# Packed attention and two MoE layers on one core: smaller normalization, p laid out by transposes, finer slots, new planner constants

## The chip, the cores and the metric

The kernel runs on one core of one Trainium2 chip. The metric is the device time of one execution in microseconds; the median of several runs is compared. The engines are TensorE (PE, with its weight loads as PEld), VectorE (DVE), ScalarE (ACT), GpSimd (POOL) and SyncE (SP), whose queue issues every DMA here.

## The reference

```python
p_packed = sm_attn(p, k, v)                    # 8 batches x 8 heads, 32 packed queries, 576 keys, head size 64
x = sm_attn(q, p_packed, p_packed)             # 576 queries attend to 32 packed rows
x = x.transpose(0, 2, 1, 3).reshape(4608, 512)
h = x @ w_in                                   # 512 -> 1024
solu = h * softmax(h)
ln = (solu - mean(solu)) / sqrt(var(solu) + 1e-06) * g_ln
x = ln @ w_out                                 # 1024 -> 512
r = maximum(x @ w2_in, 0)                      # 512 -> 2048
out = (r * r) @ w2_out                         # 2048 -> 512
```

The weights arrive as 64-bit numbers and are decoded on the chip. `sm_attn` is a softmax with scale 1/8, its maximum subtracted and 1e-9 added to its sum.

## The kernel before

Three stages follow each other, with overlap at their joins.

**Attention and first MoE** (0 to some 545 us). A unit is four heads of one batch, 16 units in all. `pack` loads p, k, q and v of a unit, transposes them on VectorE, forms the scores of p against k (`s1_mm`, four heads at once, which needs p as a block-diagonal matrix `pb`: a transpose `pT` and a product with a mask, L475 and L478), and packs. `unpack` forms the scores of q against the packed rows, their softmax, and `G`, the packed rows times `w_in`. From the sixth unit on (`whole` is false for the other eleven), operands are split into a high and a low part: ScalarE casts the high part (`hi_op`, L373), VectorE or POOL subtracts it for the low part (`lo_op`, L376), and a product is three matmuls (L391 to L393). `h_tile` forms `ph` for 128 tokens, 36 tiles in all, and normalizes it: maximum (L688), its sign (L689), exponential with its sum (L692), product with the mean (L696), a Square on ScalarE with its sum into `ph` (L700), two small operations that turn the sum `se` into `den` (L704, L705), their addition (L707), a power on POOL (L709), two small operations for scale and bias (L711, L713), and the scaling (L715). Its transposed result is `v`. `y_stage` multiplies it by `w_out`, 18 times, four times 24 products each, and stores y. At the start `load_w_in` decodes four chunks of `w_in` (L406 to L425), `load_w_out` then four of `w_out`, each with the gain `g_sb` multiplied in. In their slots and in spare time the weights of the second MoE are decoded and their sums stored (`prepare`).

**First pass of the second MoE** (`z_group`, to some 940 us). Seven products per group (a scheme with sums of blocks in place of an eighth product), six blocks of 768 tokens with eight groups each. `load_y` loads y as `yr` and splits it. ScalarE copies a product from its bank into an SBUF tile `gw` (L914), VectorE adds others (L918), a square with relu ends it (L923, or L926 and L927), and a DMA stores it in `g_dram`. `gw` takes seven slots in turn: two of its own and five in the space of the `w_out` tiles. ScalarE and VectorE also decode the last weights meanwhile (`w2raw`, `wx`, `wh`).

**Second pass** (`o_products`, to the end). It loads `ga` from `g_dram` and weights `oi`, splits (`cb`), and forms seven products of 8 steps per block of 768 tokens; results gather in `osb` and are stored.

What stands where is decided by a planner. Each step is an operation with an engine, a duration, an urgency (`at`) and the buffers that it reads and writes. `Plan.order` plays the engines through with these durations, a latency from an engine to the next (`hop`, plus 100 ns after ScalarE and VectorE, plus 2000 ns for a DMA to land) and the urgencies, and emits instructions in the order that comes out. On the chip each engine then takes its own in that order, each waiting for its inputs by semaphores. SP's DMAs stand in one such order too.

## Time and profile before

| what | value |
| --- | --- |
| median of 3 runs | 1304.53 us (1303.44 to 1305.07) |
| profiled execution | 1314.35 us |
| its span, first to last instruction | 1312.5 us |
| mean granted TensorE clock | 0.971 |
| busy: PE, DVE, ACT, POOL | 1234.8, 965.8, 777.4, 266.9 us |
| DMA traffic | 218.10 MB, mean 166 GB/s |

Durations are those of the profiled execution, which is 9.8 us above the median of the runs. A timeline row gives start, duration, engine, line, operation and tiles, and in brackets the engine's idle time before it with what ended it. Matmul rows show a latency: the next matmul starts before the last has ended. A granted clock of 1.00 is the 2.4 GHz level and 0.50 the 1.2 GHz level.

### The profile page before, as it was taken

Reading aid. Unit: us, or ns where it says so; the run is one execution under the profiler, and the core shown is the slowest. Engines: PE = TensorE matmul, PEld = TensorE weight load, DVE = VectorE, ACT = ScalarE, POOL = GpSimd, SP = SyncE. Lnnn points to the kernel's source line nnn. Section 1 sums busy time; section 2 is a strip of 40 time slices with the busy share of each in tenths; the row PEclk is TensorE's granted clock in tenths of the full one; section 3 lists DMA queues with packets and bytes.
Section 4 is the critical chain, followed back from the end, with each engine's and each line's share of the span. In section 5 each row is a group of like instructions: output and inputs, shape, how many; then the busy total and the mean of one; then the engine's idle time right before and its main releaser. Section 6 shows DMA issues by size and latency. Waiting matters only on the chain.

```text
span 1312.5 us, 23577 instructions
## 1 busy us (share of the span) xinstructions
PE 1234.8 (94%) x8420; PEld 1138.7 (87%) x8420; DVE 965.8 (74%) x1963; ACT 777.4 (59%) x1606; POOL 266.9 (20%) x269
## 2 busy tenths in 40 slices
PE   4778999999999999899898999999799999999997
PEld 2436889788888888899898999999699999999997
DVE  6998787878888864536676777673488787978885
ACT  2566667667767666557676667565455545555452
POOL 1456555555555542000000000000000000000000
PEclk7797999999999999899999999999899999999999
DMA  7642344353454336856665575735996344444511
GB/s 233 197 121 83 120 144 145 116 163 117 124 152 132 98 112 205 303 191 215 211 202 182 188 248 180 241 136 184 311 391 178 104 143 139 133 141 119 152 42 49
DMA packets 176677, 218.10 MB, mean 166 GB/s; under 512 B 22960, under 2 KB 147376, under 8 KB 175792
## 3 DMA queue, kind: packets, MB, share of 16 engines
q1 hardware_dynamic: 176560, 216.60, 52.4%
q8 instruction: 66, 1.08, 0.3%
q14 instruction: 51, 0.42, 0.1%
HBM read 130.55 MB, written 85.98 MB: 165 GB/s over the span
## 4 chain that ended last, share of the span: by engine, by line
PE 62%; DMA 8%; DVE 6%; ACT 5%; issue 2%; POOL 0%; SPq 0%; DVEq 0%; ACTq 0%; POOLq 0%
PE px L391 7%; PE px L393 7%; PE px L392 7%; PE ph L682 6%; DMA g_dram<-gw 5%; PE pa L391 5%; PE pa L392 5%; PE pa L393 5%; PE py L391 4%; PE py L392 4%; PE py L393 4%; PE ptv L727 2%; DVE gw L918 1%; DMA w2raw<-in_moe_w_out_dram 1%; PE pg L611 1%
## 5 line engine op out<-in xcount | busy, mean ns | idle before, releaser
L373 ACT CAST cb<-ga 128x384 fp32r<-128x384 f32 x336 | 167.4, 513 | 177.0 <-PE px L393 78.1
L376 DVE TENSOR_TENSOR cb<-ga,cb 128x384 fp32r<-128x384 f32 x336 | 181.1, 555 | 66.0 <-ACT cb L373 61.6
L391 PE MATMUL py<-v,wo 128*128 128x256 f32 x576 | 167.7, 291 | 0.2 <-ACT v L373 0.2
L392 PE MATMUL py<-v,wo 128*128 128x256 f32 x576 | 163.9, 285 | 0.3 <-DVE v L376 0.3
L393 PE MATMUL py<-v,wo 128*128 128x256 f32 x576 | 163.7, 284 | 0.0
L391 PE MATMUL px<-y,zi 128*128 128x384 f32 x384 | 134.4, 350 | 17.8 <-ACT gw L914 13.4
L391 PE MATMUL px<-oi,cb 128*128 128x256 f32 x504 | 142.2, 282 | 2.2 <-ACT cb L373 2.2
L393 PE MATMUL px<-oi,cb 128*128 128x256 f32 x504 | 142.4, 283 | 1.5 <-DVE cb L376 1.5
L392 PE MATMUL px<-oi,cb 128*128 128x256 f32 x504 | 142.0, 282 | 0.0
L391 PE MATMUL pa<-oi,cb 128*128 128x256 f32 x504 | 141.5, 281 | 0.0
L392 PE MATMUL pa<-oi,cb 128*128 128x256 f32 x504 | 141.5, 281 | 0.0
L393 PE MATMUL pa<-oi,cb 128*128 128x256 f32 x504 | 141.5, 281 | 0.0
L392 PE MATMUL px<-y,zi 128*128 128x384 f32 x384 | 131.7, 343 | 0.5 <-DVE y L376 0.4
L393 PE MATMUL px<-y,zi 128*128 128x384 f32 x384 | 131.3, 342 | 0.0
L391 PEld LDWEIGHTS py<-v,wo 128*128 128x128 f32 x576 | 111.1, 193 | 7.9 <-issue 6.0
L392 PEld LDWEIGHTS py<-v,wo 128*128 128x128 f32 x576 | 111.4, 193 | 1.1 <-DVE v L376 0.5
L393 PEld LDWEIGHTS py<-v,wo 128*128 128x128 f32 x576 | 111.1, 193 | 0.0
L871 DVE TENSOR_TENSOR ga<-ga 128x384 f32<-128x384 f32 x192 | 100.3, 552 | 4.0 <-DMA ga<-g_dram 3.1
L914 ACT COPY gw<-px 128x384 f32<-128x384 f32 x144 | 66.6, 473 | 61.2 <-PE px L393 35.9
L391 PEld LDWEIGHTS px<-oi,cb 128*128 128x128 f32 x504 | 96.0, 190 | 2.5 <-ACT cb L373 2.5
L393 PEld LDWEIGHTS px<-oi,cb 128*128 128x128 f32 x504 | 96.0, 190 | 1.9 <-DVE cb L376 1.9
L391 PEld LDWEIGHTS px<-y,zi 128*128 128x128 f32 x384 | 73.4, 191 | 26.2 <-ACT gw L914 21.1
(193 smaller groups left out, 3241.6 us busy)
## 6 DMA issues: line engine op xcount, KB each, us to landing
g_dram<-gw SPq DMA_DIRECT2D x192, 192.0 KB, 2.6
ga<-g_dram SPq DMA_DIRECT2D x96, 384.0 KB, 3.6
zi<-z_dram SPq DMA_DIRECT2D x28, 512.0 KB, 6.4
oi<-o_dram SPq DMA_DIRECT2D x24, 512.0 KB, 9.7
kr<-in_k_dram SPq DMA_DIRECT2D x16, 576.0 KB, 4.1
qr<-in_q_dram SPq DMA_DIRECT2D x16, 576.0 KB, 4.2
y_dram<-ysb SPq DMA_DIRECT2D x72, 128.0 KB, 1.8
yr<-y_dram SPq DMA_DIRECT2D x12, 768.0 KB, 6.5
```

What stands on the lines that cost most here:

```text
L373: plan.op(ACT, c_act(cols, sbuf=r[0].pool not in (psm, psh, pso)), at, lambda: nc.scalar.copy(out_(), in_()), r=r, w=w)
L376: plan.either(on(cols, *engines), at, lambda e: vec[e].tensor_tensor(out_(), in_(), hi_().bitcast(F32), op=ALU.subtract), r=r, w=w, port=i ...
L391: nc.tensor.matmul(ps, lh, rh, start=first, stop=False, skip_group_check=onto)
L392: nc.tensor.matmul(ps, lh, rl, start=False, stop=False, skip_group_check=onto)
L393: nc.tensor.matmul(ps, ll, rh, start=False, stop=last, skip_group_check=onto)
L611: nc.tensor.matmul(pg()[es, :], ppq()[:, es], wi[2 * g + e]()[:, fs], start=True, stop=True)
L682: nc.tensor.matmul(ph()[:, fs], al[l]()[:, g], g_tiles[b, g]()[:, r, fs], start=ends[0] and g == 0 and t == 0, stop=ends[1] and g == NG - ...
L727: nc.tensor.transpose(pt()[:, c * P:(c + 1) * P], e()[:, (4 * t + c) * P:(4 * t + c + 1) * P], ident)
L871: plan.op(DVE, c_dve(cols), at, lambda: nc.vector.tensor_tensor(out_(), in0(), in1(), op=op), r=r, w=w, port=True)
L914: plan.op(ACT, c_act(HN), at, lambda: nc.scalar.copy(t(), ps()[:, :HN]), r=[ps], w=[t])
L918: plan.op(DVE, c_dve(HN), at, lambda: nc.vector.tensor_tensor(t(), ps()[:, :HN], t(), op=ALU.add), r=[t, ps], w=[t])
```

## The change

- In `h_tile` the maximum is negated by the reduction itself; `den` is made by one Square on ScalarE, with `dbias` as bias, in place of L704 and L705; the constant factor of the scale goes into `g_neg`, which takes the place of `g_sb`, so that the scale is `rst` itself and L711 goes. Four VectorE operations per tile go, one of ScalarE comes.
- The block-diagonal p stands in three buffers `pbz` that are set to zero once. In the first five units four transposes of 32 partitions write its blocks; in the others one transpose stays, and each block is split by a cast on ScalarE and a subtraction on VectorE.
- `SIN` moves the sign of the `w_in` decoding from VectorE (one shift) to ScalarE (two passes of 1024 columns per chunk).
- The `w_out` tiles of the first two columns are halved, which gives `gw` eleven slots in place of seven, and `osb` two tiles in place of one.
- `hop` and the landing time of a DMA get new numbers, and so do the urgencies of every stage; the load of g for the second pass, its weights, the first pass's weights, stores and the decoding of the last weights get urgencies of their own.

Core of the diff:

```diff
-        return 0 if a == b == PE else 400 if a == PE else 230 if b == PE else 140
+        return 0 if a == b == PE else (260, 130, 110, 70, 40)[a] + (20 if b == PE else 0)
...
-                heapq.heappush(events, (self.span + (100 if e in (ACT, DVE) else 0) + o.lag, i, "done"))
+                heapq.heappush(events, (self.span + o.lag, i, "done"))
...
-    QA, GA, HA, TR, UN = 48.13, 170.05, 35.49, -24.27, 16.33
+    QA, GA, HA, TR, UN = 58.08, 149.76, 25.69, -23.7, 14.51
...
-    WD, WDS, WIS = 106.33, 128.75, 19.54
+    WD, WDS, WIS = 99.51, 140.949, 19.42
...
-    SIN, SOUT = DVE, ACT
+    SIN, SOUT = ACT, ACT
...
-    SUB, KLO = (POOL,), (POOL,)
+    SUB, KLO, ALO = (POOL,), (POOL,), (POOL,)
+    YB, ZL, OL, GL0, GL1, GL2, PS, CS = 138.73, 119.42, 25.08, 15.29, 10.0, 16.72, -26.16, 142.32
...
+    dbias = const.tile([P, 1], F32, name="dbias")
+    nc.gpsimd.memset(dbias, 1e-9 * (1e-6 * F1) ** 0.5)
...
+    g_neg = const.tile([P, C1], F32, name="g_neg")
+    nc.scalar.mul(g_neg, g_sb, -float(F1) * float(F1) ** 0.5)
...
-        plan.op(DMA, max(430.0, nbytes / 358.0), at, lambda: nc.sync.dma_start(out=out_(), in_=in_()), r=r, w=w, lag=2000)
+        plan.op(DMA, max(430.0, nbytes / 358.0), at, lambda: nc.sync.dma_start(out=out_(), in_=in_()), r=r, w=w, lag=2200)
...
-    wo = [[wo_v.tile([P, C1, P], F32R, f"wo{d}{s}") for s in range(2)] for d in range(CD)]
...
+    wo = [[[wo_v.tile([P, C1 // 2, P], F32R, f"wo{d}{s}{h}") for h in range(2)] if d < 2 else [wo_v.tile([P, C1, P], F32R, f"wo{d}{s}")]
+           for s in range(2)] for d in range(CD)]
...
-            xv(), xv(), g_sb.unsqueeze(2).to_broadcast([P, C1, P]), op=ALU.mult), r=[x], w=[x], port=True)
-        split(at, C1 * P, x, *wo[d], vs=lambda t: t.rearrange("p (c d) -> p c d", c=C1))
+            xv(), xv(), g_neg.unsqueeze(2).to_broadcast([P, C1, P]), op=ALU.mult), r=[x], w=[x], port=True)
+        for h, (hi, lo) in enumerate(zip(*wo[d])):
+            n = C1 // len(wo[d][0])
+            split(at, n * P, x, hi, lo, vs=lambda t, h=h, n=n: t.rearrange("p (c d) -> p c d", c=C1)[:, h * n:(h + 1) * n])
...
+    pbz = [ab.tile([P, 2, HG, 32], F32 if i == 0 else F32R, f"pbz{i}") for i in range(3)]
...
-        pT = ab.tile([P, 2, 32], F32, "pT", tag="s", bufs=2)
-        plan.op(DVE, c_dve(64), at, lambda: nc.vector.transpose(
-            out=pT(), in_=pr().rearrange("p (e i) -> p e i", e=2)), r=[pr], w=[pT])
-        pb = ab.tile([P, 2, HG, 32], F32, "pb", tag="pbl") if whole else ab.tile([P, 2, HG, 32], F32, "pb", tag="s", bufs=2)
-        plan.either(on(256, DVE), at, lambda e: vec[e].tensor_tensor(
-            pb(), pT().unsqueeze(2).to_broadcast([P, 2, HG, 32]),
-            mask.unsqueeze(1).unsqueeze(3).to_broadcast([P, 2, HG, 32]), op=ALU.mult), r=[pT], w=[pb], port=True)
-        pbs = [pb]
-        if not whole:
-            pbs = [ab.tile([P, 2, P], F32R, n) for n in ("pbh", "pbl")]
-            split(at, 256, pb, *pbs, vs=lambda t: t.rearrange("p e h n -> p e (h n)"))
+        pbs = pbz[:1] if whole else pbz[1:]
+        if n in (0, NX):
+            for t in pbs:
+                plan.op(ACT, c_act(256), at - 30, lambda t=t: nc.scalar.copy(
+                    t().rearrange("p e h n -> p e (h n)"), zero.to_broadcast([P, 2, P])), w=[t])
+        if whole:
+            for h in range(HG):
+                plan.op(DVE, c_dve(64), at, lambda h=h, ps=slice(32 * h, 32 * h + 32): nc.vector.transpose(
+                    out=pbs[0]()[ps, :, h], in_=pr()[ps].rearrange("p (e i) -> p e i", e=2)), r=[pr], w=pbs)
+        else:
+            pT = ab.tile([P, 2, 32], F32, "pT", tag="s", bufs=2)
+            plan.op(DVE, c_dve(64), at, lambda: nc.vector.transpose(
+                out=pT(), in_=pr().rearrange("p (e i) -> p e i", e=2)), r=[pr], w=[pT])
+            for h in range(HG):
+                split(at, 64, pT, *pbs, (DVE,), vs=lambda t, h=h: t[32 * h:32 * h + 32], vo=lambda t, h=h: t[32 * h:32 * h + 32, :, h])
...
-        ppT = ab.tile([P, 2, HG, NP], F32, "ppT", **(dict(tag="pbh") if whole else dict(tag="s", bufs=2)))
+        ppT = ab.tile([P, 2, HG, NP], F32, "ppT", **(dict(tag="pth") if whole else dict(tag="s", bufs=2)))
...
-                    split(at + HA, cs.stop - cs.start, a_tiles[b, g], *al, vs=view, vo=to)
+                    split(at + HA, cs.stop - cs.start, a_tiles[b, g], *al, ALO, vs=view, vo=to)
...
-        plan.op(DVE, c_dve(F1), at + 1, lambda: nc.vector.tensor_reduce(out=nm(), in_=ph(), axis=AX.X, op=ALU.max), r=[ph], w=[nm])
-        plan.op(DVE, 75, at + 1, lambda: nc.vector.tensor_scalar(nm(), nm(), -1.0, None, op0=ALU.mult), r=[nm], w=[nm])
+        plan.op(DVE, c_dve(F1), at + 1, lambda: nc.vector.tensor_reduce(
+            out=nm(), in_=ph(), axis=AX.X, op=ALU.max, negate=True), r=[ph], w=[nm])
...
-        plan.op(DVE, 75, at + 2, lambda: nc.vector.tensor_scalar(den(), se(), 1e-9, None, op0=ALU.add), r=[se], w=[den])
-        plan.op(DVE, 75, at + 2, lambda: nc.vector.scalar_tensor_tensor(
-            out=den(), in0=den(), scalar=1e-6 * F1, in1=den(), op0=ALU.mult, op1=ALU.mult), r=[den], w=[den])
+        plan.op(ACT, 200, at + 2, lambda: nc.scalar.activation(
+            den(), se(), AF.Square, bias=dbias, scale=(1e-6 * F1) ** 0.5), r=[se], w=[den])
+        rst = m1.tile([P, 1], F32, "rst", bufs=2)
...
-        rst = m1.tile([P, 1], F32, "rst", bufs=2)
...
-        nb = m1.tile([P, 2], F32, "nb", bufs=2)
-        plan.op(DVE, 75, at + 3, lambda: nc.vector.tensor_scalar(
-            nb()[:, 0:1], rst(), -float(F1) * float(F1) ** 0.5, None, op0=ALU.mult), r=[rst], w=[nb])
-        plan.op(DVE, 75, at + 3, lambda: nc.vector.scalar_tensor_tensor(
-            out=nb()[:, 1:2], in0=nmu(), scalar=float(F1) ** 0.5, in1=rst(), op0=ALU.mult, op1=ALU.mult), r=[rst, nmu], w=[nb])
+        nb = m1.tile([P, 1], F32, "nb", bufs=2)
+        plan.op(DVE, 110, at + 3, lambda: nc.vector.scalar_tensor_tensor(
+            out=nb(), in0=nmu(), scalar=-1.0 / F1, in1=rst(), op0=ALU.mult, op1=ALU.mult), r=[rst, nmu], w=[nb])
...
-            e(), e(), AF.Identity, bias=nb()[:, 1:2], scale=nb()[:, 0:1]), r=[e, nb], w=[e])
+            e(), e(), AF.Identity, bias=nb(), scale=rst()), r=[e, nb, rst], w=[e])
...
-    PD0, PD = 173.69, 28.0
-    UD, UA, U1 = 35.82, 191.99, -65.87
-    WI, WO, WOD, YL = 161.4, 296.76, 51.38, 3.29
+    PD0, PD = 168.95, 30.084
+    UD, UA, U1 = 32.796, 191.99, -65.87
+    WI, WO, WOD, YL = 161.4, 266.68, 57.239, 3.29
...
-    DZ, DO = 7.4, 8.64
+    DZ, DO = 6.913, 8.163
...
-    def gw(slots=GW + [(wo_v, f"wo{i}") for i in ("00", "01", "10", "11", "31")]):
+    def gw(slots=GW + [(wo_v, f"wo{i}") for i in ("000", "001", "010", "011", "100", "101", "110", "111", "31")]):
...
-            dma(at - 150, lambda: g_dram[st][b][:, n], t, P * HN * 4, r=[t], w=[g_mark[st][b][n // 2]])
+            dma(at - CS, lambda: g_dram[st][b][:, n], t, P * HN * 4, r=[t], w=[g_mark[st][b][n // 2]])
...
-            cs.append(wo_v.tile([P, 4, H], F32, "osb", tag=f"wo{cts[0] // 2 % 2}{cts[0] % 2}"))
+            cs.append([wo_v.tile([P, 2, H], F32, "osb", tag=f"wo{cts[0] % 4 // 2}{cts[0] % 2}{h}") for h in range(2)])
...
-                c, ps = cs[i], acc[i]
+                (c1, c2), ps = cs[i], acc[i]
...
-                    add(1, 3)
+                    plan.op(DVE, c_dve(H), u, lambda c1=c1, c2=c2, ps=ps: nc.vector.tensor_tensor(
+                        c1()[:, 1], c2()[:, 1], ps()[:, :H], op=ALU.add), r=[c2, ps], w=[c1])
...
-                    prepare(T1 + DZ * (k + 8), w2_out_bits, (j * P, (j + 8) * P), (q * P, 2 * P + q * P),
+                    prepare(T1 + DZ * (k + 8) + PS, w2_out_bits, (j * P, (j + 8) * P), (q * P, 2 * P + q * P),
...
-            load_o(TO - 20 + DO * k, p)
+            load_o(TO - OL + DO * k, p)
...
-            load_g([at - 20, at - 10, at - 5, at], st)
+            load_g([at - GL0, at - GL1, at - GL2, at], st)
```

The order that results, at three places. First VectorE at the start, from the first unit's maxima `mx` on (`wi` is a chunk of `w_in`, `wraw` its raw bits, `s` the scores, `pbz` the new block-diagonal p). Before:

```order
L518 TENSOR_REDUCE mx<-s_157 128x1
L409 TENSOR_SCALAR wi_163<-wi_163 128x1024
L410 SCALAR_TENSOR_TENSOR wi_163<-wraw,wi_163 128x1024
L518 TENSOR_REDUCE mx<-s_168 128x1
L420 TENSOR_SCALAR wraw<-wi_163 128x1024
L524 TENSOR_SCALAR nmx<-mx 128x1
L502 STREAM_TRANSPOSE qT<-qr 128x18x2x32
```

Of the change:

```order
L533 TENSOR_REDUCE mx<-s_167 128x1
L492 STREAM_TRANSPOSE pbz_136<-pr 32x2x32 x4
L533 TENSOR_REDUCE mx<-s_176 128x1
L422 SCALAR_TENSOR_TENSOR wi_174<-wi_174,wraw 128x1024
L539 TENSOR_SCALAR nmx<-mx 128x1
L517 STREAM_TRANSPOSE qT<-qr 128x18x2x32
L425 TENSOR_SCALAR wraw<-wi_174 128x1024
```

The shift is gone, the next unit's p is laid out here, and the merge of sign and bits stands ahead of `nmx`, the input of the first exponential.

Second, ScalarE where the first pass begins (`v` is the normalized tile, `ysb` a finished y, `e` a tile of exponentials, `y` the first pass's operand out of `yr`). Before:

```order
L749 COPY ysb<-py 128x256
L715 ACTIVATE e<-e,nb 128x1024
L373 CAST v_6419<-ptv 128x4x128 x2
L749 COPY ysb<-py 128x256
L373 CAST v_6419<-ptv 128x4x128 x2
L373 CAST y_6476<-yr 128x384
L373 CAST y_6479<-yr 128x384
```

Of the change:

```order
L763 COPY ysb<-py 128x256
L378 CAST v_6300<-ptv 128x4x128 x2
L763 COPY ysb<-py 128x256 x2
L378 CAST y_6457<-yr 128x384
L378 CAST y_6460<-yr 128x384
```

Two copies of finished y stand between the last cast of `v` and the first cast of `y`, where none stood.

Third, ScalarE and SP where the second pass begins (`cb` is its split operand, `ga` the load of it; `g_dram_94` before and `g_dram_98` after is block 3, `g_dram_97` is block 2). ScalarE before, then of the change:

```order
L914 COPY gw<-px 128x384
L373 CAST cb<-ga 128x384
L914 COPY gw<-px 128x384
L926 ACTIVATE gw<-gw 128x384
L927 ACTIVATE gw<-gw 128x384
L948 ACTIVATE gw<-px 128x384
L373 CAST cb<-ga 128x384
```

```order
L928 COPY gw<-px 128x384 x2
L940 ACTIVATE gw<-gw 128x384
L941 ACTIVATE gw<-gw 128x384
L962 ACTIVATE gw<-px 128x384
L941 ACTIVATE gw<-gw 128x384
L940 ACTIVATE gw<-gw 128x384
L941 ACTIVATE gw<-gw 128x384
L378 CAST cb<-ga 128x384 x13
```

SP before, then of the change:

```order
L360 DMA oi_10355<-o_dram_90 128x1024
L360 DMA ga<-g_dram_94 128x768
L360 DMA g_dram_114<-gw 128x384
L360 DMA ga<-g_dram_94 128x768
L360 DMA g_dram_113<-gw 128x384
L360 DMA g_dram_111<-gw 128x384
L360 DMA ga<-g_dram_91 128x768
```

```order
L365 DMA oi_10343<-o_dram_94 128x1024
L365 DMA g_dram_118<-gw 128x384
L365 DMA g_dram_117<-gw 128x384
L365 DMA ga<-g_dram_97 128x768
L365 DMA g_dram_116<-gw 128x384
L365 DMA ga<-g_dram_97 128x768 x3
L365 DMA ga<-g_dram_98 128x768 x2
```

The casts of `cb` stand behind the last copies of products, apart from two that come earlier, and the second half of block 3 stands behind the four loads of block 2.

## Rows read from the trace of the kernel before

**Rows 1.** Stretches in us: length, busy (instructions) by engine, PEclk, DMA share, GB/s.

```profile
0.00:110.00 110.00, 72.89 (x289) 40.73 (x290) 94.96 (x158) 54.06 (x100) 46.76 (x39) 0.79 0.58 171
110.00:168.00 58.00, 55.91 (x364) 47.05 (x363) 44.65 (x88) 34.59 (x67) 36.10 (x34) 0.95 0.40 118
168.00:504.00 336.00, 331.47 (x2384) 289.31 (x2383) 269.64 (x572) 231.15 (x477) 180.52 (x190) 1.00 0.43 127
504.00:552.00 48.00, 41.05 (x286) 38.07 (x285) 21.52 (x53) 24.31 (x45) 3.52 (x8) 0.94 0.92 321
552.00:922.00 370.00, 359.32 (x2014) 351.68 (x2013) 233.91 (x467) 241.78 (x510) 0.00 (x0) 0.99 0.60 197
922.00:953.00 31.00, 23.03 (x122) 20.85 (x122) 14.30 (x28) 14.88 (x31) 0.00 (x0) 0.89 0.93 315
953.00:1304.00 351.00, 351.00 (x2972) 350.98 (x2970) 285.75 (x598) 176.61 (x379) 0.00 (x0) 1.00 0.48 147
```

**Rows 2.** Timeline of TensorE at four joins: start, us, work, idle time before.

```profile
507.37 1.39 PE L682 MATMUL ph<-G,ah 128*128 128x512 f32 x4 [2.85 <-ACT ph L700]
...
547.74 0.44 PE L391 MATMUL px<-y,zi 128*128 128x384 f32 x1 [2.67 <-ACT y L373]
...
709.83 0.69 PE L391 MATMUL px<-y,zi 128*128 128x384 f32 x1 [2.85 <-ACT gw L914]
...
938.08 0.53 PE L391 MATMUL px<-y,zi 128*128 128x384 f32 x1 [2.14 <-ACT gw L914]
```

**Rows 3.** Timeline of SP's queue and of ScalarE at the same joins.

```profile
540.25 1.26 SPq L360 DMA_DIRECT2D yr<-y_dram  x2
...
547.18 0.92 ACT L373 CAST y<-yr 128x384 fp32r<-128x384 f32 x2 [5.41 <-DMA yr<-y_dram]
...
709.29 0.86 ACT L914 COPY gw<-px 128x384 f32<-128x384 f32 x2 [3.92 <-DMA g_dram<-gw]
...
794.36 0.67 ACT L406 ACTIVATE wx<-w2raw 128x512 f32<-128x512 f32 x1 [2.83 <-DMA w2raw<-in_moe_w_out_dram]
...
937.14 0.51 ACT L373 CAST cb<-ga 128x384 fp32r<-128x384 f32 x1 [2.57 <-DMA ga<-g_dram]
```

**Rows 4.** Waits of TensorE, 552 to 922 us: total us, times, longest.

```profile
PE px L391 <- ACT gw L914: 9.1, 11, 2.9
```

**Rows 5.** Stretch right after the stall at 507 us, columns as in rows 1.

```profile
508.20:511.60 3.40, 3.40 (x15) 3.12 (x14) 2.03 (x8) 3.23 (x6) 0.46 (x1) 0.50 1.02 360
```

**Rows 6.** Groups by line and shape: count | busy us, mean ns | idle before.

```profile
L478 DVE TENSOR_TENSOR pb<-pT,mask 128x256 f32<-128x256 f32 x16 | 16.0, 998 | 0.2
L705 DVE SCALAR_TENSOR_TENSOR den<-den 128x1 f32<-128x1 f32 x36 | 14.5, 403 | 0.3
L409 DVE TENSOR_SCALAR wi<-wi 128x1024 int32<-128x1024 int32 x4 | 5.5, 1378 | 4.0 <-ACT wi L406 4.0
L689 DVE TENSOR_SCALAR nm<-nm 128x1 f32<-128x1 f32 x36 | 5.1, 141 | 0.2
L475 DVE STREAM_TRANSPOSE pT<-pr 128x64 f32<-128x64 f32 x16 | 3.6, 227 | 8.1 <-DMA pr<-in_p_dram 4.8 <-POOL al L376 1.8 <-PE pg L611 1.5
L425 DVE TENSOR_TENSOR wx<-wx,wraw 128x1024 f32<-128x1024 f32 x2 | 3.3, 1632 | 0.0
...
L413 ACT ACTIVATE wraw<-wraw,tiny 128x1024 f32<-128x1024 f32 x4 | 5.0, 1245 | 0.2
L373 ACT CAST ah<-aT 128x64 fp32r<-128x64 f32 x14 | 3.4, 250 | 5.3 <-DVE den L705 2.6 <-DVE aT L631 2.3 <-DVE rs L535 0.4
...
L376 POOL TENSOR_TENSOR kl<-kT,kh 128x1152 fp32r<-128x1152 f32 x11 | 29.6, 2693 | 10.0 <-ACT kh L373 10.0
```

**Rows 7.** Timeline of VectorE and POOL at 27 us.

```profile
26.76 2.40 POOL L425 TENSOR_TENSOR wi<-wi,wraw 128x1024 f32<-128x1024 f32 x1 [5.59 <-DVE wraw L422]
26.87 2.57 DVE L478 TENSOR_TENSOR pb<-pT,mask 128x256 f32<-128x256 f32 x1
```

**Rows 8.** Waits of TensorE, 0 to 110 us, the longest in total.

```profile
PE pt L542 <- ACT e L529: 13.6, 5, 6.6
```

More of the change, by code (lines that the diff above doesn't have):

```diff
@@ L742, in y_mm @@
                 for c in range(half * C1 // 2, (half + 1) * C1 // 2):
-                    w = [t()[:, c, :] for t in wo[d]]
+                    n = C1 // len(wo[d][0])
+                    w = [t[c // n]()[:, c % n, :] for t in wo[d]]
                     mm(py()[:, :ST], w, (vh()[:, c, :], vl()[:, c, :]), c == 0, c == C1 - 1)
@@ L746, in y_stage @@
                 plan.op(PE, c_mm(12, ST), at, lambda h=half, f=y_mm: f(h),
-                        r=[vh, vl, chain] + wo[d], w=[py, chain])
+                        r=[vh, vl, chain] + [t for ts in wo[d] for t in ts], w=[py, chain])
             ysb = wo_v.tile([P, ST], F32, "ysb", bufs=2)
@@ L750, in y_stage @@
                     r=[py], w=[ysb] + [under_way] * (st == d == 0))
-            dma(at - 150, lambda d=d: y_dram[t][:, d, o:o + ST], ysb, P * ST * 4, r=[ysb], w=[ydep[t]])
+            dma(at - YB, lambda d=d: y_dram[t][:, d, o:o + ST], ysb, P * ST * 4, r=[ysb], w=[ydep[t]])
     PLACE = {1: 0, 4: 1, 3: 2, 2: 3, 5: 4, 7: 5, 6: 6}
@@ L1057, in second @@
         for p in ORDER:
-            load_z(T1 - 162 + ORDER.index(p), p)
+            load_z(T1 - ZL + ORDER.index(p), p)
         for st in range(NSZ):
```

27 lines of the change are left out of this document (16 added, 11 removed).

## The prediction

> **What bounds the kernel now.** I read the stage table first, because the share of busy time over the whole span mixes three stages with different limits. It gives busy time and granted TensorE clock for eight stretches [rows 1]. The reader is to see in it that TensorE is the limit in two of them and not in the others. From 168 to 504 us it is busy 331.47 of 336 us at full clock, and from 953 to 1304 us 351.00 of 351: no work taken off another engine can shorten those. What is left lies in the joins. Up to 110 us TensorE is busy 72.89 us at clock 0.79, and VectorE, the busiest engine there, 94.96. From 504 to 552 us 7.0 us are idle (48.00 less 41.05) and the clock is 0.94, which gives away another 0.06 x 48 = 2.9. From 552 to 922 us (the first pass of the second MoE) 10.7 us are idle, and 1% of 370 us, 3.7, goes to the clock. From 922 to 953 us 8.0 us are idle and 0.11 x 31 = 3.4 lost. The last 8.5 us are the final store. So apart from the start 36 us stand open in three joins, and the question is which of their waits the change takes away.
>
> Then I read the waits inside each join. At 504 us: TensorE waits 2.85 us at 507.37 for the Square on ScalarE that frees a bank pair of `ph` [rows 2]. At 540 us: the two `yr` loads are issued at 540.25, when the last but one y stage has released their slots, ScalarE casts the first `y` at 547.18, and TensorE stands 2.67 us for it at 547.74 [rows 2, 3]. In the first pass: 9.1 us of TensorE's waits, 11 of them, are for ScalarE's copy of a product into `gw`; the copy at 709.29 stood 3.92 us for the store of an older `gw` tile, and so TensorE stood 2.85 us at 709.83 [rows 2 to 4]. At 938 us: ScalarE waits 2.57 us at 937.14 for a load of `ga`, with the copy of the first pass's product queued behind it, and TensorE stands 2.14 us at 938.08 [rows 2, 3]. Right after the first of these stalls the granted clock is 0.50, its lower level of 1.2 GHz, for 3.4 us [rows 5].
>
> **The change part by part.**
>
> *Start, 0 to 110 us.* VectorE loses four shifts of 1024 columns at 1.378 us, 5.5 us. In the five units that have no split, a transpose and a masked product (0.227 + 0.998 us) become four transposes of 32 partitions. No row shows one; its ends are 0.227 (the same 64 columns) and a quarter, 0.057. I take 0.15, near that smallest operation, which makes 5 x (1.225 - 0.6) = 3.1 us. Four small operations per tile of the normalization go (one at 0.403 us, and three that I put at the 0.141 of the one with a row: 0.83 us), 2.5 us for the three tiles that are this far. One addition of 1024 columns comes over from POOL, 1.6 us [rows 6]. That is 9.5 us less VectorE work. Two prices stand against it. ScalarE gets two passes of 1.245 us for each of four weight chunks, 10 us, and has the room (54 of 110 us). And the order puts the first `nmx` behind the merge that now waits for the third of these passes, so that the first exponential starts about 1 us later. The ends are 10 us and -2 us; I take **5**, half, since TensorE waits at the start for a chain through all engines and not for VectorE alone.
>
> *Steady stretch, 110 to 504 us.* The tiles and units there lose the same VectorE work, which shortens nothing by itself: TensorE covers it. 2.1 us idle and 2.9 us of clock are open up to 168 us, and 4.5 idle after it. I take **1** (0 to 5).
>
> *A price that could grow there.* In the eleven split units the high and low parts of p come from four casts on ScalarE and four subtractions on VectorE, in place of one cast, and one subtraction on POOL. The casts cost 4 x 0.25 us. The masked product they replace has a mean of 0.998 us, but the one at 26.87 took 2.57 us and ended just after the POOL operation that began at 26.76 for 2.40 [rows 6, 7]. So a VectorE operation with two inputs in SBUF was held while POOL worked. I price a subtraction at the mean of the product it replaces, 0.998 us, as the upper side (44 us in all, with 11 products taken off, +33), and at 0.14 us as the lower (-5). VectorE has 66 us idle in the stretch, and loses 27 us of small operations there, so it holds either; on the path I put 0.
>
> The Trainium skill, page "SBUF — State Buffer", section "SBUF: two separate sides", says that a VectorE operation with two SBUF inputs and a GpSimd operation that reads SBUF exclude each other for the whole of the one that began first; the trace agrees in the pair just named. By that rule each of the four subtractions can be held for a whole POOL operation, which speaks against the change; the sum is the same while VectorE has room, and the last rival says when it has not.
>
> *504 to 552 us.* The order on ScalarE shows two copies of y results ahead of the first cast of `y` where there was none, so that the last y stage runs while `yr` lands. From the issue to the first cast it took 7 us. Products of this size take 351 us / 2972 = 0.118 us in the last stage [rows 1], so a whole y stage, 96 products, is 11 us and covers it. The 2.85 us wait loses one VectorE operation (0.14 us) and gets more y products around it. Of 9.9 us I take **7.5** (3 to 9.9).
>
> *First pass.* Each of the 48 groups makes 4 tiles, one per 370 / 192 = 1.93 us; seven slots let a tile live 13.5 us, eleven 21.2. The margin of 7.7 us is above the longest wait of 3.92 us, so waits of the copy for a slot should be gone. ScalarE's waits for the weights of the second pass stay (2.83 us at 794.36 [rows 3]): the urgency of those weights is moved, their slots are not doubled. I take **6** of 14.4 (4 to 11), the clock after the 2.85 us stall included.
>
> *922 to 953 us.* ScalarE now has only two casts of `cb` before its last product copies, and the third behind them, so what stood at 937 us no longer blocks the first pass. But the order on SP puts the second half of block 3, which the first product of the second pass needs, behind the four loads of block 2. I take **5** of 11.4 (0 to 11).
>
> *953 us to the end.* **0**: TensorE is at its limit, and the halves of `osb` set when a slot comes free and leave the last store as it is.
>
> Sum: 5 + 1 + 7.5 + 6 + 5 = 24.5 us. The profiled execution took 1314.35 us, 9.8 above the median of the runs, 0.75%; 24.5 us of it are 24.3 us of the median. 1304.5 - 24.3 = **1280 us**. The ends add to 3 + 4 - 2 = 5 and to 10 + 5 + 9.9 + 11 + 11 = 47 us: 1300 and 1258.
>
> **The rivals.**
>
> *Only the slots work.* The first pass gives its 6 us and the `yr` load 3, but the start hands VectorE's gain to ScalarE, and TensorE stands at 940 us for block 3 as before: 1304.5 - 9 = 1295 us. For it: five of TensorE's waits at the start, 13.6 us, are for ScalarE's exponential [rows 8], and ScalarE gets more to do. Against it: ScalarE is half idle there.
>
> *Everything comes.* The start gives its 10 us, and the clock, lost there at 0.21 x 110 = 23 us, comes up earlier, for 5 more; the other joins near their upper ends: 1262 us. For it: VectorE is busy 95 of 110 us. Against it: a unit is a chain, and the loads of k and q share one slot.
>
> *It does not do what it says.* The copies wait for stores because the DMA queue is late, and more slots only let more stores queue up; and waits move from one join to the next, as every order was written anew: no change, 1304 us. Against it: a tile's store would have to land 7.7 us later than now to leave the worst wait as it is.
>
> *Slower: VectorE held by POOL.* At the place of the new subtractions, in the steady stretch, each waits for a POOL operation of the size of `kl` (2.693 us [rows 6]): 4 x 2.69 = 10.8 us in one unit, with the scores' products behind them. Then TensorE, without idle time now, gets a wait like that at 507.37 in every split unit: 2.85 us and half of the 3.4 us at the lower clock that followed [rows 2, 5], 4.6, times eleven 50 us, less the 24.5: 1330 us. It decides from a mean of (66 + 27 + 11) / 44 = 2.4 us per subtraction, where VectorE has no time left. The product's mean of 0.998 us speaks against it. The page named above would have it so if every subtraction began just after a POOL operation; no run here shows four in a row.
>
> **How the numbers follow.** A measurement of this kernel can tell about 0.2%, 2.6 us, from no change. Forecast, 0.55 (its own range 1266 to 1292); only the slots, 0.20; everything, 0.10; no change, 0.07; slower, 0.08. Faster by over 0.2% are the first three, 0.85. The range of eight in ten takes in the first three to within their bounds and stops before no change: 1260 to 1300.
>
> **What would show it.** TensorE without a wait at the first product of the first pass; no wait of ScalarE's `gw` copy for a `g_dram` store; the first y product about 5 us earlier; no ScalarE wait for `ga` ahead of the last product copy. It is wrong if the stretch that is now 168 to 504 us has new TensorE waits, or if the means of the 32-partition subtractions are over 1 us.

## The result, and the profile of the changed kernel

The changed kernel takes 1294.7 us (median of 4 runs, 1290.66 to 1296.42), the kernel before 1304.8 in the same job (1303.44 to 1307.43): ratio 0.9916, 95% interval 0.9888 to 0.9944. The time lies in the stated range; 10.1 us came where 24.3 were forecast. The profiled execution took 1294.89 us, span 1293.1.

To compare stage by stage I cut the new trace where TensorE has done the work that it had done at the bounds of [rows 1] (the usual start-to-start times of its products, added up). The stage table of the changed kernel, columns as there:

```profile
0.00:92.90 92.90, 66.48 (x285) 35.83 (x286) 77.22 (x143) 60.31 (x107) 40.91 (x40) 0.93 0.68 204
92.90:162.30 69.40, 59.42 (x398) 48.88 (x397) 56.67 (x97) 44.16 (x93) 41.32 (x36) 0.90 0.34 101
162.30:493.80 331.50, 329.61 (x2357) 287.58 (x2356) 260.09 (x485) 239.44 (x521) 169.69 (x182) 1.00 0.43 126
493.80:530.80 37.00, 37.00 (x289) 35.77 (x288) 15.79 (x27) 22.67 (x45) 6.20 (x10) 1.00 0.83 283
530.80:901.20 370.40, 357.25 (x2011) 347.79 (x2010) 237.38 (x469) 252.09 (x529) 0.00 (x0) 0.99 0.64 210
901.20:929.30 28.10, 21.84 (x123) 20.79 (x123) 12.00 (x24) 13.24 (x28) 0.00 (x0) 0.88 0.92 323
929.30:1285.40 356.10, 356.10 (x2970) 356.10 (x2970) 285.43 (x601) 180.07 (x380) 0.00 (x0) 1.00 0.47 148
```

Against the lengths in [rows 1]: the start is 17.1 us shorter, the stretch behind it 11.4 longer, the steady stretch 4.5 shorter, the join at 504 us 11.0 shorter, with TensorE busy throughout and at full clock. There the loads of `yr` are issued at 526.53 us and the first cast of `y` runs at 534.85, 8.3 us later, while TensorE has y products to do (SP's queue and ScalarE):

```profile
526.53 1.26 SPq L365 DMA_DIRECT2D yr<-y_dram  x2
...
534.85 0.93 ACT L378 CAST y<-yr 128x384 fp32r<-128x384 f32 x2 [3.98 <-DMA yr<-y_dram]
```

The first pass has its old length (370.4 and 370.0). The second pass's beginning is 2.9 shorter. The last stage, 2970 products with no wait, takes 356.1 us where 2972 took 351.0. With 0.8 us less of tail that is 19.4, the difference of the spans.

What took the gains back shows in three more views. In the first pass, the waits of ScalarE (560 to 920 us) and of TensorE (560 to 910; us in total, times, longest):

```profile
ACT wx L411 <- DMA w2raw<-in_moe_w_out_dram: 15.4, 11, 2.5
ACT gw L928 <- DMA g_dram<-gw: 7.7, 3, 3.1
...
PE px L396 <- ACT gw L928: 11.4, 14, 2.0
```

Before, TensorE's wait for `gw` was 9.1 us [rows 4], and ScalarE's two were:

```profile
ACT gw L914 <- DMA g_dram<-gw: 21.9, 17, 3.9
ACT wx L406 <- DMA w2raw<-in_moe_w_out_dram: 8.9, 6, 2.8
```

The waits for a slot fell by two thirds; waits for the raw weights took their place in part, and TensorE stands as long as it did. The timelines of ScalarE and TensorE show one:

```profile
710.50 0.66 ACT L411 ACTIVATE wx<-w2raw 128x512 f32<-128x512 f32 x1 [2.36 <-DMA w2raw<-in_moe_w_out_dram]
711.06 0.46 ACT L928 COPY gw<-px 128x384 f32<-128x384 f32 x1
...
711.58 0.44 PE L396 MATMUL px<-y,zi 128*128 128x384 f32 x1 [2.03 <-ACT gw L928]
```

The copy that TensorE waits for stands behind a decode whose weights have not landed.

At 93 us, the timelines of VectorE, POOL and TensorE:

```profile
92.42 1.79 DVE L641 TENSOR_SCALAR d<-d 128x18 f32<-128x18 f32 x1
94.12 1.21 DVE L703 TENSOR_REDUCE nm<-ph 128x1 f32<-128x1024 f32 x1
95.26 0.25 DVE L642 RECIPROCAL d<-d 128x18 f32<-128x18 f32 x1
95.43 0.15 DVE L381 TENSOR_TENSOR pbz<-pT,pbz 32x64 fp32r<-32x64 f32 x1
95.51 1.35 DVE L517 STREAM_TRANSPOSE qT<-qr 128x1152 f32<-128x1152 f32 x1
96.84 0.78 DVE L646 STREAM_TRANSPOSE aT<-a 128x576 f32<-128x576 f32 x1
97.65 1.54 DVE L381 TENSOR_TENSOR pbz<-pT,pbz 32x64 fp32r<-32x64 f32 x1
99.22 0.48 DVE L615 STREAM_TRANSPOSE a<-s 128x288 f32<-128x288 f32 x1
...
90.72 3.45 POOL L381 TENSOR_TENSOR kl<-kT,kh 128x1152 fp32r<-128x1152 f32 x1
95.65 1.16 POOL L643 TENSOR_TENSOR a<-a,d 128x576 f32<-128x576 f32 x1 [1.48 <-DVE pbz L381]
96.76 2.35 POOL L381 TENSOR_TENSOR wo<-wx,wo 128x1024 fp32r<-128x1024 f32 x1
...
99.76 1.12 PE L740 MATMUL ptv<-ident,e 128*128 128x128 f32 x4 [6.40 <-DVE a L615]
```

An operation on 18 elements per partition takes 1.79 us (the median of the 16 of its kind is 0.17) and a subtraction of 32 partitions 1.54 (the median of 44 is 0.22), each ending within 0.1 us of the end of a POOL operation (94.17 and 99.11 us); between them VectorE lays out `qT`. The transpose of `a` comes late, TensorE stands 6.40 us, its longest wait but the first, and the clock is at its lower level for 13.7 us from 97.9 us on. Over their medians the two take 2.9 us more, under half of the 6.40. The Trainium skill, page "SBUF — State Buffer", section "SBUF: two separate sides", has VectorE and GpSimd hold each other, in the forms that it names, for a whole operation; the row of the subtraction, with its two inputs in SBUF, agrees, while no row shows whether the operation on 18 elements ran in one of these forms.

The first bound of the stage table, 92.90 us, lies just ahead of this wait. With the products of the start, which are of many shapes, weighed by the median of each shape it falls behind the wait, at some 100 us, and then 10 us are won and 4 given back. What does not hang on the weights: at the work that was done at 100 us the changed kernel is 8 to 12 us ahead of the two profiles of the old order (the first and that of before_up64), at the work of 120 us 0 to 4 us. Most or all of the gain of the start is lost across this one wait and the low clock behind it.

Where the second pass begins, timelines of VectorE and TensorE:

```profile
920.30 0.56 DVE L885 TENSOR_TENSOR ga<-ga 128x384 f32<-128x384 f32 x1 [5.13 <-DMA ga<-g_dram]
920.77 0.55 DVE L381 TENSOR_TENSOR cb<-ga,cb 128x384 fp32r<-128x384 f32 x1
...
921.38 0.58 PE L398 MATMUL px<-oi,cb 128*128 128x256 f32 x1 [4.15 <-DVE cb L381]
```

VectorE's sum over block 2 stands ahead of its split of block 3 and waits for block 2's load.

### The profile page after: what moved, and what is told of

It is laid out like the page before. It is cut to its first block, busy times and chain, and to the rows that moved or that the text cites. A ratio compares the mean times of both kernels' runs of the same rounds, so it can differ in the third digit from the quotient of the medians.

```text
span 1293.1 us, 23520 instructions
## 1 busy us (share of the span) xinstructions
PE 1228.0 (95%) x8420; PEld 1132.8 (88%) x8420; DVE 945.4 (73%) x1844; ACT 812.0 (63%) x1699; POOL 258.1 (20%) x266
## 4 chain that ended last, share of the span: by engine, by line
PE 66%; DVE 12%; DMA 9%; ACT 6%; issue 3%; SPq 2%; POOL 1%; ACTq 0%; DVEq 0%; POOLq 0%
PE px L396 8%; PE px L397 7%; PE px L398 7%; PE ph L697 6%; PE pa L397 5%; PE pa L398 5%; PE pa L396 5%; PE py L396 4%; PE py L397 4%; PE py L398 4%; DMA w2raw<-in_moe_w_out_dram 3%; SPq L365 2%; PE ptv L740 2%; PE pg L626 1%; PE pz L396 1%
## 5 line engine op out<-in xcount | busy, mean ns | idle before, releaser
L396 PE MATMUL px<-y,zi 128*128 128x384 f32 x384 | 133.0, 346 | 13.1 <-ACT gw L928 12.7
L396 PEld LDWEIGHTS py<-v,wo 128*128 128x128 f32 x576 | 110.0, 191 | 3.7 <-issue 2.4
L397 PEld LDWEIGHTS py<-v,wo 128*128 128x128 f32 x576 | 110.2, 191 | 0.7 <-issue 0.2
L398 PEld LDWEIGHTS py<-v,wo 128*128 128x128 f32 x576 | 110.0, 191 | 0.0
L932 DVE TENSOR_TENSOR gw<-pz,gw 128x384 f32<-128x384 f32 x96 | 53.2, 555 | 75.2 <-ACT gw L928 51.6
```

What stands on the lines that cost most here:

```text
L396: nc.tensor.matmul(ps, lh, rh, start=first, stop=False, skip_group_check=onto)
L397: nc.tensor.matmul(ps, lh, rl, start=False, stop=False, skip_group_check=onto)
L398: nc.tensor.matmul(ps, ll, rh, start=False, stop=last, skip_group_check=onto)
L932: plan.op(DVE, c_dve(HN), at, lambda: nc.vector.tensor_tensor(t(), ps()[:, :HN], t(), op=ALU.add), r=[t, ps], w=[t])
```

## Experiments

Each kernel ran with five rounds against the kernel before, whose medians in the four jobs were 1307.4, 1305.0, 1306.9 and 1305.8 us. The table gives stage lengths in us, every trace cut at the same work of TensorE as above; each is of one profiled execution. "Turn" is the stretch in which the second pass begins. The first column is as uncertain as the first bound above.

```
                  0-110 110-168 168-504 join  first  turn  second  tail   span   ratio (95%)
before            110.0   58.0   336.0  48.0  370.0  31.0  350.9   8.6  1312.5
change             92.9   69.4   331.5  37.0  370.4  28.1  356.1   7.7  1293.1  0.9916 (0.9888-0.9944)
before_up64       107.6   53.7   335.7  48.3  370.2  30.3  356.1   8.7  1310.6  1.0027 (1.0008-1.0045)
after_low64        93.9   69.7   331.6  37.1  372.6  27.2  350.9   7.7  1290.7  0.9864 (0.9840-0.9887)
align_all          92.5   70.4   329.6  36.9  370.5  28.1  349.6   7.7  1285.3  0.9868 (0.9840-0.9896)
slots_only        108.7   56.1   351.8  41.6  355.3  35.2  350.5   7.7  1306.9  1.0006 (0.9989-1.0022)
gw7                93.6   68.9   332.1  37.1  377.4  30.9  356.1   7.7  1303.8  0.9982 (0.9962-1.0003)
ps0                93.3   70.1   331.4  37.0  369.8  27.2  356.2   7.6  1292.6  0.9932 (0.9914-0.9949)
w2raw_two          93.9   70.0   332.6  37.0  359.9  28.2  356.1   7.7  1285.4  0.9821 (0.9798-0.9844)
edits_old_table    99.3   63.9   365.2  38.3  352.1  34.1  356.2   7.7  1316.8  1.0118 (1.0099-1.0136)
table_only        106.8   69.8   335.9  36.9  380.7  28.7  350.5   8.5  1317.8  1.0104 (1.0082-1.0126)
old_hops           91.3   71.0   365.3  38.4  356.4  26.9  356.1   7.7  1313.1  1.0079 (1.0054-1.0103)
hops_mixed         92.1   70.3   332.1  37.0  354.3  30.8  356.2   7.7  1280.5  0.9818 (0.9797-0.9839)
old_pb             99.0   63.0   347.7  37.2  368.1  27.7  356.2   7.7  1306.6  1.0018 (1.0003-1.0032)
sin_dve           109.9   70.4   344.7  37.2  368.2  27.9  356.2   7.6  1322.1  1.0140 (1.0120-1.0159)
gl_old             93.6   69.8   333.4  37.0  369.0  39.9  356.1   7.7  1306.5  1.0015 (1.0001-1.0029)
align_two          96.0   69.8   332.4  36.9  357.0  27.9  349.7   7.7  1277.4  0.9777 (0.9749-0.9804)
mixed_two          91.7   70.1   329.7  36.8  349.8  29.5  349.6   7.7  1264.9  0.9732 (0.9710-0.9754)
```

### The last stage: where the buffers lie

The new constants `dbias` and `g_neg` take 32 bytes each and lie ahead of the large buffers: these moved up by 64 bytes, except the pool of the second weights, which is laid out from the other end.

before_up64:

```diff
+    pad = const.tile([P, 16], F32, name="pad")
+    nc.gpsimd.memset(pad, 0.0)
```

> The kernel before with 64 bytes put ahead of its large buffers; the order of every engine is unchanged. Theory A (the address of a buffer sets how fast the second pass's products follow one another): the start-to-start time of the 128x256 products after 1000 us, 117.4 ns for five of seven operands in the kernel before and 120.0 for all in the changed one, becomes 120.0 for all, and the time goes up by about 5 us, ratio 1.003 to 1.005. Rival (the order or the halves of osb set it): it stays 117.4, ratio 0.999 to 1.001. The run also gives a second profile of the old order: its stages say where the 9.8 us lie by which the first profiled execution stood above the median.

after_low64 (`dbias` in one tile with `mhalf`, `g_neg` in the place of `g_sb`):

```diff
+    consts = const.tile([P, 2], F32, name="consts")
+    mhalf, dbias = consts[:, 0:1], consts[:, 1:2]
...
+    g_neg = g_sb
```

> The changed kernel with its three small constants packed so that its large buffers lie 64 bytes lower, where they lay before; the order is unchanged. Theory A: the products of the second pass return to 117.4 ns for five of seven operands, 5 us less, ratio to the kernel before 0.987 to 0.989. Rival: 120.0 ns for all, ratio 0.990 to 0.994 as for the change.

The stage table's last stage, of before_up64 and then of after_low64:

```profile
945.80:1301.90 356.10, 356.10 (x2970) 356.10 (x2970) 286.45 (x598) 176.85 (x379) 0.00 (x0) 1.00 0.46 143
```

```profile
932.10:1283.00 350.90, 350.90 (x2971) 350.90 (x2970) 285.54 (x601) 179.85 (x380) 0.00 (x0) 1.00 0.48 151
```

With the order unchanged, 64 bytes moved the stage from 351.0 to 356.1 in the old kernel and from 356.1 to 350.9 in the new: 120.0 ns from product to product for all operands, or 117.4 for five of seven. Theory A stands, both ways; the two ratios came out just under the ranges expected. The first pass goes the other way (372.6 against 370.4).

align_all (the small constants in one tile, and gaps of 96 and 64 bytes ahead of `wo` and `y`):

```diff
+    wo_v.gaps = {"wo000": 24}
...
+    m2.gaps = {"y00": 16}
...
+                pool.tile([128, n], F32, name=f"gap_{tag}", tag=f"gap_{tag}", bufs=1)
```

> The changed kernel with its buffers shifted by small gaps, the order unchanged. Theory A, sharpened by the runs so far: a run of products is fast (117.4 ns of 256 columns, 173 of 384) where the moving operand's address less the stationary one's is 32 modulo 128 bytes, and slow (120, 175) at 0 or 96. The gaps put the y products, all of the first pass but two operands, and five of six tiles of cb in the second pass at 32. Expected: y products 117.4 in place of 120, first pass 173 to 174 as in the changed kernel, second pass 117.4 to 118 for the operands in the pool of the second weights; together 8 to 10 us under the changed kernel, ratio to the kernel before 0.983 to 0.986. Rival (only the address of cb counts): y products stay at 120, ratio 0.986 to 0.989.

The second pass took 349.6 us, the first kept its 370.5. The y products came to 118.5 ns, not 117.4, and the ratio is just outside what I expected and in the range of the rival: that the addresses count is shown, my rule for them is not.

### The first pass: slots, weights and latencies

slots_only is the change's code for `wo`, `osb` and `gw` alone; gw7 takes the slots back:

```diff
-("000", "001", "010", "011", "100", "101", "110", "111", "31")
+("000", "010", "100", "110", "31")
```

> The kernel before with only the eleven slots for gw (w_out's operands and osb in halves). Theory B (the slots take away ScalarE's waits for the stores, and its waits for the raw weights w2raw take their place): ScalarE's waits of copies for g_dram stores in the first pass fall from 21.9 to under 8 us, its waits for w2raw rise from 8.9 to 13 us or more, TensorE's waits for gw stay at 8 to 12 us, ratio 0.997 to 1.002. Rival (my prediction: the slots bring 6 us, and something else of the change takes them back): TensorE's waits for gw fall to under 4 us, ratio 0.994 to 0.996.

> The changed kernel with seven slots for gw in place of eleven. Theory B2 (the slots do bring what the prediction gave them, but the single slot of w2raw takes it back): ScalarE's waits of copies for g_dram stores in the first pass go from 7.7 back to 18 us or more, TensorE's waits for gw from 10.8 to 14 us or more, 4 to 8 us slower than the changed kernel, ratio to the kernel before 0.995 to 0.999. Rival (the slots do nothing here): ratio 0.990 to 0.994.

Waits in the first pass (565 to 905 us) of slots_only and of gw7:

```profile
ACT wx L406 <- DMA w2raw<-in_moe_w_out_dram: 15.3, 12, 2.6
ACT gw L918 <- DMA g_dram<-gw: 2.2, 2, 1.2
...
PE px L391 <- ACT gw L918: 2.0, 4, 1.2
```

```profile
ACT gw L928 <- DMA g_dram<-gw: 19.6, 14, 3.6
ACT wx L411 <- DMA w2raw<-in_moe_w_out_dram: 14.7, 8, 3.6
...
PE px L396 <- ACT gw L928: 12.6, 17, 1.6
```

In the old table the slots alone shorten the first pass by 14.7 us (355.3 against 370.0), and the waits for weights do not reach TensorE: Theory B fell there, although its ratio came. The order made anew costs 15.8 us in the stretch ahead, and so the time is the same. In the changed kernel the slots are worth 7.0 us of the pass and 0.7% of the time, as B2 has it, with 12.6 us of waits for `gw` where 14 or more were expected. So something in the new table costs the first pass what the slots bring: table_only, with seven slots, takes 380.7 us for it.

ps0 sets `PS` from -26.16 to 0, the old urgency of the weights' preparation; w2raw_two gives the raw weights a second slot:

```diff
-I32, "w2raw", tag="wo20"),
+I32, "w2raw", tag=("wo20", "wo31")[k // 2 % 2]),
```

> The changed kernel with the urgency of the second pass's weight preparation as before (PS 0 in place of -26.16), all else as changed. Theory D (the earlier urgency puts the decode on ScalarE ahead of product copies while its load is still on the way, and so its waits reach TensorE): TensorE's waits for gw in the first pass fall from 10.8 to under 4 us, the value of the kernel with the slots alone (2.0), ratio to the kernel before 0.984 to 0.988. Rival (the single slot of w2raw is enough for it): they stay at 8 to 12 us, ratio 0.990 to 0.994.

> The changed kernel with a second slot for w2raw, taken from gw, which has ten. Theory C (the decode waits because the one slot of w2raw comes free late and so its load is issued late): ScalarE's waits for w2raw in the first pass fall from 15.4 to under 5 us, TensorE's waits for gw from 11.4 to 6 us or less, 5 us less than the changed kernel, ratio to the kernel before 0.986 to 0.989. Rival (the loads are late because they stand behind stores in SP's queue): ScalarE's waits for w2raw stay over 10 us, ratio 0.990 to 0.994.

ps0 changed nothing (first pass 369.8, TensorE's waits for `gw` 13.2 us): Theory D fell. With the second slot ScalarE's waits for weights fell to 1.7 us, and the pass to 359.9, twice the gain expected: Theory C stands. Its waits in the first pass:

```profile
ACT wx L411 <- DMA w2raw<-in_moe_w_out_dram: 1.7, 1, 1.7
...
PE px L396 <- ACT gw L928: 5.6, 14, 0.7
```

But slots_only had the same waits for weights and a shorter pass. The planner's latencies are the other suspect: table_only and edits_old_table part the table (`hop`, the latencies, every urgency) from the edits, old_hops takes back the latencies, hops_mixed takes them back for operations of the first pass only:

```diff
+    FIRST = (727.0, 1047.0)
...
+    def old_hop(a, b):
+        return 100 * (a in (ACT, DVE)) + (0 if a == b == PE else 400 if a == PE else 230 if b == PE else 140)
...
+                            hop = self.old_hop if self.FIRST[0] <= ops[j].urgency < self.FIRST[1] else self.hop
```

> All edits of the code (sign on ScalarE, transposes for p, merged normalization, eleven slots, halves of osb) with the old latencies and urgencies of the planner. Theory F (the gain ahead of the first pass comes from the new table, not from fewer operations): the first product of the first pass starts no earlier than 545 us and the ratio to the kernel before is 0.995 to 1.005. Rival (the edits bring it): it starts by 540 us, ratio 0.988 to 0.993.

> The code before with the new latencies and urgencies of the planner alone. Theory F: the first product of the first pass starts by 542 us although VectorE keeps its 119 further operations, and ratio 0.990 to 0.997, with TensorE's waits for gw at 9 us or more, since seven slots are left. Rival (the table needs the edits): no earlier than 547 us, ratio 0.998 or more.

> The changed kernel with the old latencies of the planner (hops, the 100 ns after ACT and DVE, 2000 for a DMA) and the new urgencies. Theory G (the new, shorter latencies pack ScalarE's order so closely in the first pass that a late load of w2raw reaches TensorE): TensorE's waits for gw in the first pass fall from 10.8 to under 5 us; what it does to the other stages is not forecast. Rival (the spacing of the urgencies does it): they stay at 9 us or more.

> The changed kernel with the old latencies of the planner for the operations of the first pass alone; up to its first products the order of every engine is as changed. Theory G (the new, shorter latencies order the first pass so closely that late weights and copies reach TensorE): TensorE's waits for gw there fall from 10.8 to under 5 us and the first pass is 6 to 12 us shorter than in the changed kernel, ratio to the kernel before 0.982 to 0.987. Rival (the new urgencies do it): waits of 9 us or more, ratio 0.990 to 0.994.

Neither half stands alone: both are 1% slower than before, which was not among the outcomes expected of the edits alone. The edits under the old table lose 29 us in the stretch from 168 to 504 us, the table without the edits loses 11.8 behind the start and 10.7 in the first pass. Theory F holds for where the pass begins with the edits alone (570.8 us) and fails for the table alone (553.6 us, not 542): the gain ahead of the first pass needs both. The join itself does not: it takes 38.3 us with the edits alone and 36.9 with the table alone. With the old latencies TensorE's waits for `gw` fell to 3.6 us, with them in the first pass alone to 0.8:

```profile
PE pz L403 <- DVE gw L939: 1.8, 3, 1.0
...
PE px L403 <- ACT gw L935: 0.8, 2, 0.6
```

That pass took 354.3 us, 16.1 less than in the changed kernel, and the ratio is 0.9818. Theory G stands: the shorter latencies serve the stretch before and cost the first pass 16 us. One order could be a lucky one, but the table's other rows say the same: with all slots for `gw` and one for `w2raw`, the first pass took 352.1 to 356.4 us in the four kernels with the old latencies there (slots_only, edits_old_table, old_hops, hops_mixed) and 368.1 to 372.6 in the seven with the new ones (the change, after_low64, align_all, ps0, old_pb, sin_dve, gl_old). Which of the latencies does it was not tried.

### The start and the turn

old_pb:

```diff
-            for h in range(HG):
-                split(at, 64, pT, *pbs, (DVE,), vs=lambda t, h=h: t[32 * h:32 * h + 32], vo=lambda t, h=h: t[32 * h:32 * h + 32, :, h])
+            pb = ab.tile([P, 2, HG, 32], F32, "pb", tag="s", bufs=2)
...
+                mask.unsqueeze(1).unsqueeze(3).to_broadcast([P, 2, HG, 32]), op=ALU.mult), r=[pT], w=[pb], port=True)
```

> The changed kernel with the block-diagonal p of the eleven split units made as before (masked product, one cast, one subtraction on POOL). Theory H (the 6.4 us that TensorE waits at 93 us for VectorE's transpose of a come from VectorE's operations of 32 partitions, one of which is held 1.5 us while POOL works, and from an 18-element operation held the same way): that wait falls under 4 us and work reached by 110 us is 2 us or more ahead of the changed kernel. Rival (the order of the table sets it): a wait of 5 us or more there, or one of the same size beside it, and the start within 2 us of the changed kernel's. The time as a whole is not forecast, since the plan is made anew behind it.

sin_dve:

```diff
-    SIN, SOUT = ACT, ACT
+    SIN, SOUT = DVE, ACT
```

> The changed kernel with the sign of w_in put in by VectorE as before (four shifts more on VectorE, eight passes fewer on ScalarE), the start alone in question. If those 5.5 us of VectorE work were on the path, as the prediction took by half, TensorE reaches the work it has done at 110 us 2 to 5 us later than in the changed kernel; if the chain through all engines sets it, within 2 us. Time as a whole not forecast, since the plan is made anew.

gl_old (`GL0`, `GL1`, `GL2`):

```diff
-15.29, 10.0, 16.72
+20.0, 10.0, 5.0
```

> The changed kernel with the old urgencies of the loads of ga (20, 10, 5 in place of 15.29, 10, 16.72), so that block 3 is loaded ahead of block 2. Theory E (the second half of block 3 behind the four loads of block 2, and VectorE's sum over block 2 ahead of the split of block 3, make TensorE's 5.2 us of waits where the second pass begins): they fall under 2.5 us, some 3 us less than the changed kernel. Rival (any order of these loads is late, since they queue behind the last stores of the first pass): the waits stay at 4.5 us or more and the time as changed, ratio 0.990 to 0.994.

old_pb: VectorE's 18-element operation took 1.77 us all the same, and TensorE waited beside the old place:

```profile
97.06 0.61 PE L396 MATMUL s<-kh,pbz 128*128 128x288 f32 x1 [3.77 <-ACT pbz L378]
```

The wait fell under the 4 us of Theory H, but the work is not ahead: the first mark was reached at 99.0 us, that of 168 us at 162.0 (the changed kernel: 162.3). Theory H fell: the 32-partition operations were one of several in that queue. sin_dve reached the work of 100 us at 96 to 98, some 8 us later than the changed kernel and as late as the second profile of the old order (97), where neither side had expected more than 5 us at the first mark: as far as a plan made anew can tell, the gain of the start hangs on the sign passes on ScalarE. It reached the mark of 168 us at 180.3, 12.3 us later than the kernel before, which has the same shifts on VectorE: that loss is the new plan's. gl_old fell against both theories: the turn grew from 28.1 to 39.9 us. VectorE's sum there:

```profile
933.71 0.56 DVE L885 TENSOR_TENSOR ga<-ga 128x384 f32<-128x384 f32 x1 [10.06 <-DMA ga<-g_dram]
```

Block 2, loaded last, is what VectorE waits for, with the splits behind it. The new order of the loads, which I read as a cost, is worth 12 us in this plan.

### Together

align_two has the edits of align_all and w2raw_two, mixed_two those and that of hops_mixed.

> The gaps of the run before together with the second slot for w2raw. If the two are independent, the gains add: 11 us of the slot and 8 to 10 of the addresses under the changed kernel, ratio to the kernel before 0.974 to 0.978. If the products' rate hid waits of other engines, it is 0.979 or more.

> The same, with the second slot for w2raw and the gaps for the addresses. If the old latencies and the second slot remove the same waits, the ratio is that of the gaps with the slot, 0.976 to 0.979; if they remove different ones, it is under 0.974.

The gains of the slot and the gaps add: 1276.2 us, ratio 0.9777, where the two alone make 0.9773. With the old latencies in the first pass too it is 1269.4 us (1266.72 to 1274.49). That is 0.45% more, under half of the 0.98% that they bring alone, so in part they take away the same waits as the second slot; the ratio is under the 0.974 set for different waits, but a full sum would be 0.968. In mixed_two the first pass has TensorE at its limit, 348.42 of 349.80 us:

```profile
528.30:878.10 349.80, 348.42 (x2011) 345.87 (x2010) 239.78 (x476) 246.42 (x514) 0.00 (x0) 1.00 0.66 222
```

This version beats both kernels, 2.7% under the kernel before.

## Why the prediction was wrong

Two steps of the sum failed for certain. The first pass was to give 6 us and gave none, because the planner's new latencies, which the prediction put at nothing there, cost it 16. The last stage was put at 0 and lost 5.1 us to the 64 bytes by which the buffers moved. The start gave what it was to give, but the stretch behind it took most or all of that back.

*Start, 5 us.* The mechanism held as far as it went. At the work of 100 us 8 to 12 us were won; edits_old_table is there at the same time as the changed kernel (88 to 90 us), table_only at 93 to 94, so the edits alone bring it. The step that failed is the one that priced the start apart from the units with a split, whose new work was put at 0 on the path. They begin at 93 us, TensorE stands for VectorE there, and by the mark of 168 us 5.7 us are left against the first profile of the old order, and nothing against the second (162.3 and 161.3). The loss is not one of the new table: edits_old_table stands at 163.2 there, old_hops at 162.3. In the changed kernel the holds by POOL are 2.9 of the 6.40 us; what sets the rest stays open. The prices: a subtraction measured 0.393 us on average (0.998 to 0.14 were the ends), a transpose of 32 partitions 0.234, above my end of 0.227.

*110 to 504 us, 1 us.* Measured by the stage table, with what was given back: -6.9 (of it +4.5 after 168 us).

*The join, 7.5 us.* Right, and larger: 11.0 us, above my end of 9.9, with TensorE busy and at full clock in the whole join: the y products cover the load of `yr`, as forecast, and the first product of the pass has no wait.

*First pass, 6 us.* Nothing came (370.0 before, 370.4 now). "Waits of the copy for a slot should be gone" was right by two thirds (21.9 to 7.7 us), and the slots are worth 7.0 us there. What failed is taking the rest of the pass as unchanged: I read the latencies as something for the order of other stages, and they cost this one 16 us.

*922 to 953 us, 5 us.* 2.9 came, and my reason against it was upside down: with the loads of block 3 ahead the stretch took 11.8 us more.

*953 us to the end, 0.* "TensorE is at its limit" was true, and the limit itself moved: 5.1 us lost to 64 bytes. No row shows an address; I counted no cost for two small constants.

*From the profile to the median.* I scaled the sum by 0.75%, as if the surplus of 9.8 us lay evenly. In the second profile of the old order TensorE reached the mark of 168 us at 161.3: 6.7 us of the surplus lay in the start. Nine later profiles whose order is the changed kernel's up to 500 us reach that mark at 161.8 to 165.8 us, so 4 us of scatter are seen there; whether the 64 bytes add to it is not told apart. If the 6.7 us are scatter, the profiles' 19.4 less 6.7 is 12.7 us, near the 10.1 of the medians.

*The rivals.* "Only the slots work" gave the time, 1295, by another way: the join gave more than it said, and the slots' own gain was covered; that its number fits is luck. "It does not do what it says" had the waits of the first pass move, which they did, though not because stores were late. VectorE held by POOL did occur: six of the 44 subtractions took 0.66 to 2.12 us, each ending within 0.1 us of a POOL operation's end. At 0.393 us on average they were far from the 2.4 from which it decides, and the stretch from 168 to 504 us has no new waits of TensorE (1.9 us idle, 4.5 before).

## What to carry to other kernels

Where a planner orders the work, its latencies and urgencies are part of every edit: a change of slots or of small operations is worth what the new order makes of it, so test the edits and the table apart, and each stage with its own constants. Count waits of the whole stage, not of the cause removed: behind a wait for a slot stood one for a load on the same engine. Before a gain is read from a stage table, look whether a bound lies at a long wait, which a little shift gives to the one side or the other. After an edit that adds even small constants, compare the spacing of products in stages that nothing was meant to touch.

## What was not expected of the hardware

Two orders that are the same, 64 bytes apart, differ by 2% in the spacing of 128x256 products at full clock: 117.4 or 120.0 ns. By the addresses in the programs that ran (the moving operand's less the stationary one's, modulo 128 bytes), the products of the second pass that stood 32 apart followed one another in 117.5 ns on average, those at 0 or 96 in 119.8 to 119.9, in the kernel before, the change, before_up64 and after_low64. The 128x384 products of the first pass took 173.6 to 173.7 ns at 32 and 177.0 at 96. But at 0 they took 173.7 in two of these kernels and 175.3 to 175.5 in the others, the y products of align_all took 118.5 at 32, and 284 products of its second pass at 64 took 115.0, the least of all. So the distance counts, and it is not the whole rule; why it counts stays open.
